# Attention probabilities in two parts: the second part written over its source, three heads in flight, sums two heads behind

## The chip, the cores and the metric

The kernel runs on one core of one Trainium2 chip. The metric is the device time of one execution in microseconds. The core has five engines with a queue each: TensorE (PE in the profile; its weight loads are listed as PEld), VectorE (DVE), ScalarE (ACT), GpSimd (POOL) and SyncE (SP), which issues nearly all DMAs. Each engine works through its own queue in order, and queues wait for one another through semaphores.

## The reference

One transformer block on x of 2048 tokens by 1024 channels, in fp32: a memory-augmented causal attention with 32 heads of 32 channels over four segments of 512 tokens, and then a token-mixing MLP. Both are modulated by a vector computed from c. Cut to the part that the change touches:

```python
for s in range(N):                      # N = 4 segments, L = 512
    logits = einsum("bhqd,bhkd->bhqk", qs, ks) * scale + mask
    p = softmax(logits, axis=-1)
    a_dot = einsum("bhqk,bhkd->bhqd", p, vs)
    num = einsum("bhld,bhde->bhle", phi(qs), M)
    den = einsum("bhld,bhd->bhl", phi(qs), z)[..., None] + 1e-6
    outs.append(g * num / den + (1.0 - g) * a_dot)
    M = M + einsum("bhld,bhle->bhde", phi(ks), vs)
    z = z + einsum("bhld->bhd", phi(ks))
o = stack(outs) @ wo                     # heads joined
x = x + ga * o                           # h = layernorm, modulated, before
x = x + gb * (W2 gelu(W1 layernorm(x)^T + b1) + b2)^T
```

## The kernel before

**Numbers in parts.** To keep fp32 accuracy at the rate of narrower matmuls, an operand is split into a rounded first part and the rest. A large product is then three matmuls: first by first, first by second, second by first (`kv_chunk`, L187; `q_chunk`, L198; L795; L925). `split` (L117) makes the two parts: a copy on ACT and a subtraction on DVE.

**Stages.** The start (to about 60 us) computes the modulation and the first normalized segment. The attention stage follows, then the output projection (`product`, L776) with the second normalization, and then the MLP (`mix`, L910) by a seven-product scheme, which fills the rest of the run from about 1160 us. The change lies in the attention stage alone.

**The attention stage.** The work is cut into 32 items `t`: two passes, in each the eight groups of four heads, in each two segments. Each item has four heads, so there are 128 heads `n = 4t + h`. The loop at L690 runs over `n`, and each iteration issues, in this order, `scores` of head n, `maxima` of head n + 3 (LEADS), `values` of head n - VL, and one of four pieces of `project` for the item eight heads ahead (LEADP). Side work that is planned for an iteration (weight splits, normalized token tiles, the modulation's other rows) follows, some of it held behind a marked instruction of head n on the same engine (`behind`, L504).

`project` (L380): pieces 0 and 1 each multiply half of the segment's tokens by the weights of k and v, 48 matmuls of 256 columns, into a bank of the tag pj (two banks), and copy k and v out (L400, L401, on ACT). A third copy from the same bank, L406, rounds v to bf16 into the tile `vp`; after piece 1 a DVE subtraction (L408) makes the rest, `r1`. Piece 2 transposes k, projects q, splits both into `sg` and, for the memory, computes phi of q and k. Its DMAs (`stack`, L370) put each head's parts of q and k beside each other in `sk`. Piece 3 stacks the fourth head, makes v's second part (L442, ACT) and third part (L443, DVE), and runs `memory` (L446), which reads and updates M and z.

`maxima` (L473): the masked scores of one head, three banks in turn of the tag s1 (two banks), each reduced by DVE to row maxima (L485); for each pair of heads the maxima are transposed, split and sent by DMA into two further rows of `sk` (L498).

`scores` (L512): the transposed scores with the maxima already subtracted by those rows, three banks of the tag s2 (two banks), and an exponential of each on ACT (L520, L523, L527) into `p32`, 1280 fp32 columns. POOL clears the upper triangles (L530). ACT rounds all of it to fp16, the first part (L532), and POOL subtracts that from p32, in two halves of 640 columns, into the second part (L534).

`values` (L536): ten blocks for the first part (97 columns: a column of ones for the row sums, and v's three parts) and ten for the second part (65 columns) are summed in one bank, the only one of the tag pv. DVE inverts the sums (L551), adds the parts (L553) and scales (L555), and POOL adds the memory's share (L558). After the fourth head the item is transposed, copied (L565) and stored (L566) in `oT`, from which L779 loads the operands of the output projection.

**Buffers.** Until now p32 has two buffers (5,120 bytes a partition each), and the two parts share the tile `ph` with two buffers (5,120 bytes each). A p32 buffer is free when POOL has subtracted, a ph buffer when TensorE has summed. `vp` has three buffers, `v32` one, `r1` one of its own.

**What sets the order.** The program gives each engine's instructions and their data; the framework's planner simulates the program with a cost model before the run and fixes the order on each queue: by the order of the program, with instructions further on drawn forward when those ahead are not ready in that simulation. On the chip each queue then runs in that order.

Of the kernel before, what the change touches and what calls it, by code (L numbers as in the profile page):

```python
# [7 lines left out]
F32 = mybir.dt.float32  # L8
F32R = mybir.dt.float32r
F16 = mybir.dt.float16  # L10
BF16 = mybir.dt.bfloat16
AF = mybir.ActivationFunctionType
ALU = mybir.AluOpType
# [5 lines left out]
P = 128  # L19
# [8 lines left out]
NV = 97  # L28
FT = F // P
LEADP, LEADS, NSK = 8, 3, 8  # L30
XB = 4
VL = 1
PHB = 2
P32B = 2
ML0 = 36
HB = 3
WO0 = 65
# [6 lines left out]
def attention_and_mlp(ctx, tc, x, wq, wkv, wo, beta, w1, b1, w2, b2, c, wm_a, wm_b, out):  # L44
    nc = tc.nc
    V, A, G, T, SY = nc.vector, nc.scalar, nc.gpsimd, nc.tensor, nc.sync
# [17 lines left out]
    a = par.__enter__()  # L64
# [257 lines left out]
    for i in range(2):  # L322
        ps = bank("s2", 2, f"scps{i}")
# [20 lines left out]
    pj = prj.__enter__()  # L344
    late = tc.tile_pool(name="late", bufs=1, reuse_waits="tile")
    b = late.__enter__()
# [33 lines left out]
    def project(t, piece):  # L380
        pr, g, seg = its[t]
        if piece == 0:
            st[t] = {}
        w = W[pr, g]
        hp = [hpages[seg, ct] for ct in range(NK)]
        d = st[t]
        if piece in (0, 1):
            if piece == 0:
                d["k32"] = pj.tile([P, 4, 128], F32, tag="k32", bufs=1, name=f"k32_{t}")
                d["v32"] = pj.tile([P, 4, 132], F32, tag="v32", bufs=1, name=f"v32_{t}")  # L390
                G.memset(d["v32"][:, :, 128:132], 1.0)
            half = piece
            k32, v32 = d["k32"], d["v32"]
            if t:
                ps = two_tiles(bank("pj", 2, f"nps{t}_{half}"))
                for k in range(NK):
                    kv_chunk(w, hp[k], half, k, ps)
            else:
                ps = two_tiles(first[half])
            A.copy(k32[:, 2 * half:2 * half + 2], ps[:, :, 0:128])  # L400
            A.copy(v32[:, 2 * half:2 * half + 2, 0:128], ps[:, :, 128:256])  # L401
            if half == 0:
                d["vp"] = b.tile([P, 4, 4, NV], BF16, tag="vp", bufs=3, name=f"vp{t}")
                G.memset(d["vp"][:, :, :, 0:1], 1.0)
                d["r1"] = pj.tile([P, 4, 4, 32], F32, tag="r1", bufs=1, name=f"r1_{t}")
            A.copy(d["vp"][:, 2 * half:2 * half + 2, :, 1:33], ps[:, :, 128:256].rearrange("p a (h e) -> p a h e", h=4))  # L406
            if half:
                V.tensor_tensor(d["r1"], v32[:, :, 0:128].rearrange("p a (h e) -> p a h e", h=4), d["vp"][:, :, :, 1:33],  # L408
                                op=ALU.subtract)
        elif piece == 2:  # L410
            k32 = d["k32"]
            d["sg"] = sg = pj.tile([P, 4, L], F32R, tag="sg", bufs=1, name=f"sg{t}")
            ps = bank("pj", 2, f"kps{t}")
            for i in range(4):
                T.transpose(ps[:, 128 * i:128 * i + 128], k32[:, i], ident)
            split(sg[:, 2:4], ps, A, V)
            if t:
                ps = bank("pj", 2, f"qps{t}")
                for k in range(NK):
                    q_chunk(w, hp[k], k, ps)  # L420
            else:
                ps = first[2]
            split(sg[:, 0:2], ps, A, V)
            if seg:
                r = pj.tile([P, L], F32, tag="tmp", bufs=2, name=f"rq{t}")
                A.activation(r, ps, AF.Relu, scale=-1.0)
                A.activation(r, r, AF.Exp, scale=-1.0)
                d["pq"] = pj.tile([P, L], F32, tag="pq", bufs=1, name=f"pq{t}")
                V.scalar_tensor_tensor(d["pq"], ps, 0.0, r, op0=ALU.max, op1=ALU.add)
            if seg < 3:  # L430
                r = pj.tile([P, L], F32, tag="tmp", bufs=2, name=f"rk{t}")
                kf = k32.rearrange("p a n -> p (a n)")
                A.activation(r, kf, AF.Relu, scale=-1.0)
                A.activation(r, r, AF.Exp, scale=-1.0)
                d["pk"] = pj.tile([P, 4, 128], F32, tag="pk", bufs=1, name=f"pk{t}")
                V.scalar_tensor_tensor(d["pk"].rearrange("p a n -> p (a n)"), kf, 0.0, r, op0=ALU.max, op1=ALU.add)
            for h in range(3):
                stack(t, h)
        else:
            stack(t, 3)  # L440
            vp, r1 = d["vp"], d["r1"]
            A.copy(vp[:, :, :, 33:65], r1)  # L442
            V.tensor_tensor(vp[:, :, :, 65:97], r1, vp[:, :, :, 33:65], op=ALU.subtract)  # L443
            memory(t)
# [56 lines left out]
    marks = {}  # L501
# [10 lines left out]
    def scores(t, h):  # L512
        d = st[t]
        n = 4 * t + h
        q, k = d["sk", h][:, 0], d["sk", h][:, 1]
        p32 = r_.tile([P, 1280], F32, tag="p32", bufs=P32B, name=f"p32_{t}_{h}")
        d["ph", h] = ph = r_.tile([P, 2, 1280], F16, tag="ph", bufs=PHB, name=f"ph{t}_{h}")
        b0 = bank("s2", 2, f"a0_{t}_{h}")
        T.matmul(b0, k[:, 0:128], q, start=True, stop=True)  # L519
        A.activation(p32[:, 0:512], b0, AF.Exp, scale=SCALE, bias=shift)  # L520
        b1_ = bank("s2", 2, f"a1_{t}_{h}")
        T.matmul(b1_[:, 0:384], k[:, 128:256], q[:, 128:512], start=True, stop=True)  # L522
        A.activation(p32[:, 512:896], b1_[:, 0:384], AF.Exp, scale=SCALE, bias=shift)  # L523
        b2_ = bank("s2", 2, f"a2_{t}_{h}")
        T.matmul(b2_[:, 0:128], k[:, 384:512], q[:, 384:512], start=True, stop=True)
        T.matmul(b2_[:, 128:384], k[:, 256:384], q[:, 256:512], start=True, stop=True)  # L526
        A.activation(p32[:, 896:1280], b2_[:, 0:384], AF.Exp, scale=SCALE, bias=shift)  # L527
        for base, step in ((0, 512), (896, 128)):
            w = bass.AP(tensor=p32.tensor, offset=p32.offset + base, ap=[p32.ap[0], [step, 2], [1, 128]])
            G.affine_select(w, w, pattern=[[0, 2], [1, 128]], compare_op=ALU.is_ge, fill=0.0, base=0,  # L530
                            channel_multiplier=-1)
        marks[n, "A"] = A.copy(ph[:, 0], p32)  # L532
        for c in (slice(0, 640), slice(640, 1280)):
            marks[n, "G"] = G.tensor_tensor(ph[:, 1, c], p32[:, c], ph[:, 0, c], op=ALU.subtract)  # L534

    def values(t, h):  # L536
        pr, g, seg = its[t]
        d = st[t]
        am, ph = d["am"], d["ph", h]
        pv = bank("pv", 1, f"pv{t}_{h}").rearrange("p (a n) -> p a n", a=4)  # L540
        col = {0: lambda i: 128 * i, 1: lambda i: 512 + 128 * (i - 1), 2: lambda i: 1024 + 128 * (i - 2),
               3: lambda i: 896}
        n = 0
        for part, w in ((0, NV), (1, 65)):
            for i in range(4):
                for j in range(i + 1):
                    o = col[j](i)
                    T.matmul(pv[:, i, 0:w], ph[:, part, o:o + 128], d["vp"][:, j, h, 0:w], start=(n == 0),  # L548
                             stop=(n == 19), skip_group_check=True)
                    n += 1  # L550
        V.reciprocal(pv[:, :, 0], pv[:, :, 0])  # L551
        red = r_.tile([P, 4, 32], F32, tag="red", bufs=2, name=f"red{t}_{h}")
        V.tensor_reduce(red, pv[:, :, 1:97].rearrange("p a (c e) -> p a e c", c=3), axis=AX.X, op=ALU.add)  # L553
        ah = am[:, :, 32 * h:32 * h + 32]
        V.scalar_tensor_tensor(red if seg else ah, red, gate[:, 1, 4 * g + h:4 * g + h + 1],  # L555
                               pv[:, :, 0:1].to_broadcast([P, 4, 32]), op0=ALU.mult, op1=ALU.mult)
        if seg:
            G.tensor_tensor(ah, ah, red, op=ALU.add)  # L558
        if h < 3:
            return  # L560
        ps = bank("ms", 1, f"ops{t}")
        for i in range(4):
            T.transpose(ps[:, 128 * i:128 * i + 128], am[:, i], ident)
        ot = r_.tile([P, L], F32, tag="ot", bufs=1, name=f"ot{t}")
        A.copy(ot, ps)  # L565
        SY.dma_start(oT[g, :, L * seg:L * seg + L], ot)  # L566
        del st[t]
# [47 lines left out]
    with tc.issue_after(last_wm.ins):  # L615
        _, exp, _, normed_v = seg_load(1)
# [25 lines left out]
    r_ = right.__enter__()  # L642
# [32 lines left out]
    for g in range(2, NG):  # L675
        n = 8 * g - 13
# [5 lines left out]
    for j in range(32):  # L682
        n = ML0 + 2 * j + (8 if j >= 8 else 0)
        later(n, lambda j=j: mod_fetch(j), n + (2 if j < 8 else 1), lambda r, j=j: mod_late(j, r), "V")
    plan(WO0 - 3, lambda: spread(gaw, 0))
    for i in range(8):
        n = WO0 + WOS * i
        later(n, lambda i=i: wo_fetch(i), n + 1, lambda r, i=i: wo_split(i, r), "G")

    for n in range(-LEADS, 4 * NI + VL):  # L690
        at(scores, n)
        at(maxima, n + LEADS)
        at(values, n - VL)
        m = n + LEADP
        if 0 <= m + 4 < 4 * NI:
            t = (m + 4) // 4
# [12 lines left out]
        if 4 * NI - 5 <= m < 4 * NI + 3:  # L709
            i = m - 4 * NI + 5  # L710
# [21 lines left out]
    w = cw_pool.__enter__()  # L732
# [120 lines left out]
    for products, tt in (((0, 1), 0), ((2,), 1), ((3, 4, 8), 8), ((9,), 9), ((10,), 2), ((11,), 10), ((12,), 3),  # L853
# [5 lines left out]
        for i in products:  # L859
            if i > 1:  # L860
                f = product(i)
# [283 lines left out]
```

## Time and profile before

| what | us |
| --- | --- |
| median of three runs | 2234.29 |
| fastest of them | 2233.22 |
| the profiled execution, its own time | 2231.97 |
| its span, first to last instruction | 2230.3 |
| TensorE busy in the span | 2194.8 (98%) |
| DVE, ACT, POOL busy | 1675.3, 1136.8, 721.0 |

One of the three runs took 4396.86 us, which the median leaves aside. All times that are read from the trace belong to the one profiled execution; its own time lies 1.7 us above its span. The busy time of TensorE is partly modelled, since matmuls are pipelined, so that its idle time in a stage tells more than its busy share. A row of a view by groups names line, engine, operation, tiles and shapes, then the count, the busy us, the mean ns of one, and the engine's idle time just before with what ended it.

### The profile page before, as it was taken

How to read it: one execution, taken by the hardware profiler on the slowest of the kernel's cores; microseconds unless marked ns; L12 is line 12 of the kernel's file. 1: busy time of each engine (PE TensorE's matmuls, PEld its weight loads, DVE VectorE, ACT ScalarE, POOL GpSimd, SP SyncE). 2: the span in 40 equal slices, each digit the busy share in tenths (PEclk: the TensorE clock that was granted, in tenths of full speed). 3: DMA queues.
4: the chain of work that ended last, by engine and by line, in shares of the span. 5: the costliest groups of instructions: out<-in, count | busy, mean ns of one | idle time of the engine just before them, and what ended most of it. 6: DMA issues, size and time to landing. Idle time of an engine off the chain costs nothing.

```text
span 2230.3 us, 38268 instructions
## 1 busy us (share of the span) xinstructions
PE 2194.8 (98%) x13786; PEld 1885.9 (85%) x13786; DVE 1675.3 (75%) x3762; ACT 1136.8 (51%) x2082; POOL 721.0 (32%) x831
## 2 busy tenths in 40 slices
PE   8999999999999999999999999999999999999999
PEld 5889898889989989888888888888888888888887
DVE  7677677766767777655858766888888886969687
ACT  5477777756666656645636533533334242424232
POOL 2176666656766767654001200033330000000000
PEclk9999999999999999999999999999999999999999
DMA  7657565697656566765654586655556541414134
GB/s 285 191 170 212 161 191 155 202 293 220 187 165 199 178 199 181 214 189 180 218 198 178 223 322 258 245 221 221 206 204 224 204 146 62 151 57 146 57 123 151
DMA packets 175185, 423.05 MB, mean 190 GB/s; under 512 B 17524, under 2 KB 71828, under 8 KB 166036
## 3 DMA queue, kind: packets, MB, share of 16 engines
q1 hardware_dynamic: 174996, 420.61, 57.4%
q8 instruction: 109, 1.79, 0.3%
q14 instruction: 80, 0.66, 0.1%
HBM read 244.62 MB, written 125.06 MB: 166 GB/s over the span
## 4 chain that ended last, share of the span: by engine, by line
PE 87%; DVE 5%; DMA 3%; ACT 2%; POOL 2%; issue 1%; SPq 0%; ACTq 0%; DVEq 0%; POOLq 0%
PE mx L925 47%; PE nps L194 12%; PE po L795 7%; PE qps L202 7%; PE pv L548 3%; PE a L519 1%; POOL ph L534 1%; PE sz L483 1%; PE sx L483 1%; PE rd L455 1%; PE a L522 1%; PE sy L483 1%; PE up L465 1%; PE a L526 1%; ACT ph L532 1%
## 5 line engine op out<-in xcount | busy, mean ns | idle before, releaser
L925 PE MATMUL mx<-bU,sp 128*128 128x512 f32 x2352 | 534.2, 389 | 0.9 <-DVE ac L932 0.9
L925 PEld LDWEIGHTS mx<-bU,sp 128*128 128x128 f32 x2352 | 441.4, 188 | 93.2 <-issue 1.3
L194 PE MATMUL nps<-wv,h 128*128 128x256 f32 x3072 | 437.2, 282 | 1.3 <-DVE h L124 0.7
L121 ACT CAST sp<-wr 128x384 fp32r<-128x384 f32 (+2 forms) x408 | 217.3, 545 | 432.7 <-PE mx L925 355.4
L534 POOL TENSOR_TENSOR ph<-p,ph 128x640 f16<-128x640 f32 x256 | 381.2, 1510 | 155.1 <-ACT ph L532 150.8
L925 PE MATMUL mx<-bA,sp 128*128 128x512 f32 x1764 | 430.5, 389 | 0.0
L194 PEld LDWEIGHTS nps<-wv,h 128*128 128x128 f32 x3072 | 404.6, 189 | 8.7 <-DVE h L124 2.0
L925 PEld LDWEIGHTS mx<-bA,sp 128*128 128x128 f32 x1764 | 331.2, 188 | 68.6
L124 DVE TENSOR_TENSOR sp<-wr,sp 128x384 fp32r<-128x384 f32 (+2 forms) x408 | 259.7, 647 | 29.1 <-ACT sp L121 28.8
L932 DVE TENSOR_TENSOR ac<-mx,ac 128x512 f32<-128x512 f32 x280 | 189.7, 686 | 83.9 <-PE mx L925 83.5
L202 PE MATMUL qps<-h,wq 128*128 128x512 f32 x768 | 200.5, 403 | 0.4
L532 ACT CAST ph<-p 128x1280 f16<-128x1280 f32 x128 | 160.9, 1259 | 41.7 <-POOL p L530 41.3
L795 PE MATMUL po<-wo,ots 128*128 128x512 f32 x768 | 179.8, 390 | 0.6 <-DVE x L798 0.6
L795 PEld LDWEIGHTS po<-wo,ots 128*128 128x128 f32 x768 | 143.6, 188 | 30.1 <-DVE x L798 0.9
L202 PEld LDWEIGHTS qps<-h,wq 128*128 128x128 f32 x768 | 143.9, 193 | 29.0 <-ACT vp L406 1.4
L925 PE MATMUL mx<-bB,sp 128*128 128x512 f32 x588 | 164.0, 389 | 0.0
L530 POOL TENSOR_SCALAR_AFFINE_SELECT p<-p 128x256 f32<-128x256 f32 x256 | 121.3, 484 | 103.1 <-ACT p L527 51.8
L548 PE MATMUL pv<-vp,ph 128*128 128x97 bf16 (+1 forms) x2560 | 142.0, 201 | 6.5 <-DVE red L555 3.1
L548 PEld LDWEIGHTS <-ph 128*128 128x128 f16 x2560 | 113.9, 98 | 28.1 <-issue 13.3
L925 PEld LDWEIGHTS mx<-bB,sp 128*128 128x128 f32 x588 | 110.4, 188 | 22.9
L485 DVE CUSTOM_DVE_ANT_0 sx<-sx,mask 128x128 f32<-128x128 f32 (+1 forms) x256 | 93.7, 366 | 41.8 <-PE sx L483 39.5
L932 DVE TENSOR_TENSOR cc<-mx,cc 128x512 f32<-128x512 f32 x140 | 94.9, 684 | 39.6 <-PE mx L925 39.3
(207 smaller groups left out, 3149.7 us busy)
## 6 DMA issues: line engine op xcount, KB each, us to landing
sk<-sg SPq DMA_DIRECT2D x384, 128.0 KB
wr<-in_w_dram SPq DMA_DIRECT2D x28, 1024.0 KB
wr<-in_w_dram SPq DMA_DIRECT2D x32, 768.0 KB
bstu<-ucd SPq DMA_DIRECT2D x28, 768.0 KB
wsp<-wv SPq DMA_DIRECT2D x32, 512.0 KB
rawm<-in_wm_b_dram SPq DMA_DIRECT2D x32, 512.0 KB
wv<-wsp SPq DMA_DIRECT2D x32, 512.0 KB
pcd<-cc SPq DMA_DIRECT2D x14, 1024.0 KB
```

What stands on the lines that cost most here:

```text
L121: last_hi[0] = A.copy(hi, src)
L124: return lo_eng.tensor_tensor(lo, src, hi.bitcast(F32), op=ALU.subtract)
L194: T.matmul(ps[:, aa], h[:, j, 128 * tt:128 * tt + 128], wt[:, i, o:o + 256], start=(n == 0), stop=(n >= 6 * NK - 2), skip_group_check=True)
L202: T.matmul(ps, wt[:, i, o:o + 128], h[:, j], start=(k + n == 0), stop=(3 * k + n == 3 * NK - 1))
L485: marks[4 * t + h - LEADS, "V"] = V.tensor_tensor_reduce(o, o, mask[:, 384 - 128 * i:], 1.0, -3.0e38, op0=ALU.add, op1=ALU.max, accum_out= ...
L530: G.affine_select(w, w, pattern=[[0, 2], [1, 128]], compare_op=ALU.is_ge, fill=0.0, base=0, channel_multiplier=-1)
L532: marks[n, "A"] = A.copy(ph[:, 0], p32)
L534: marks[n, "G"] = G.tensor_tensor(ph[:, 1, c], p32[:, c], ph[:, 0, c], op=ALU.subtract)
L548: T.matmul(pv[:, i, 0:w], ph[:, part, o:o + 128], d["vp"][:, j, h, 0:w], start=(n == 0), stop=(n == 19), skip_group_check=True)
L795: T.matmul(ps, os_[:, i, P * ct:P * ct + P], wop[ct, nh][:, j], start=(n == 0), stop=(n == 3 * NK - 1))
L925: T.matmul(ps, ops[q][:, i, P * k:P * k + P], b[:, j], start=(m == 0 and first), stop=(m == 3 * nk - 1), skip_group_check=True)
L932: V.tensor_tensor(d, ps, d, op=ALU.add)
```

## The change

VL goes from 1 to 2: `values` of a head is issued two iterations after its `scores`. The second part of the probabilities is no longer a tile half of its own: POOL writes it, as fp16, over the first half of the bytes of the p32 buffer that it is reading. p32 and the first part have three buffers each (5,120 and 2,560 bytes a partition). A p32 buffer is therefore free when TensorE has summed the head.

v's three bf16 parts are all made in piece 3 of `project`, from the fp32 copy `v32` in SBUF: the memset of the ones, one ACT copy of all four token tiles instead of two from the PSUM bank, and the subtraction. `r1` takes a buffer of the tag tmp, which has two and is shared with the scratch of phi.

```diff
-VL = 1
-PHB = 2
-P32B = 2
+VL = 2
...
-            if half == 0:
-                d["vp"] = b.tile([P, 4, 4, NV], BF16, tag="vp", bufs=3, name=f"vp{t}")
-                G.memset(d["vp"][:, :, :, 0:1], 1.0)
-                d["r1"] = pj.tile([P, 4, 4, 32], F32, tag="r1", bufs=1, name=f"r1_{t}")
-            A.copy(d["vp"][:, 2 * half:2 * half + 2, :, 1:33], ps[:, :, 128:256].rearrange("p a (h e) -> p a h e", h=4))
-            if half:
-                V.tensor_tensor(d["r1"], v32[:, :, 0:128].rearrange("p a (h e) -> p a h e", h=4), d["vp"][:, :, :, 1:33],
-                                op=ALU.subtract)
...
             stack(t, 3)
-            vp, r1 = d["vp"], d["r1"]
+            v = d["v32"][:, :, 0:128].rearrange("p a (h e) -> p a h e", h=4)
+            vp = d["vp"] = b.tile([P, 4, 4, NV], BF16, tag="vp", bufs=3, name=f"vp{t}")
+            r1 = pj.tile([P, 4, 4, 32], F32, tag="tmp", bufs=2, name=f"r1_{t}")
+            G.memset(vp[:, :, :, 0:1], 1.0)
+            A.copy(vp[:, :, :, 1:33], v)
+            V.tensor_tensor(r1, v, vp[:, :, :, 1:33], op=ALU.subtract)
             A.copy(vp[:, :, :, 33:65], r1)
...
-        p32 = r_.tile([P, 1280], F32, tag="p32", bufs=P32B, name=f"p32_{t}_{h}")
-        d["ph", h] = ph = r_.tile([P, 2, 1280], F16, tag="ph", bufs=PHB, name=f"ph{t}_{h}")
+        p32 = r_.tile([P, 1280], F32, tag="p32", bufs=3, name=f"p32_{t}_{h}")
+        hi, lo = r_.tile([P, 1280], F16, tag="ph", bufs=3, name=f"ph{t}_{h}"), p32.bitcast(F16)[:, 0:1280]
+        d["ph", h] = hi, lo
...
-        marks[n, "A"] = A.copy(ph[:, 0], p32)
+        marks[n, "A"] = A.copy(hi, p32)
         for c in (slice(0, 640), slice(640, 1280)):
-            marks[n, "G"] = G.tensor_tensor(ph[:, 1, c], p32[:, c], ph[:, 0, c], op=ALU.subtract)
+            marks[n, "G"] = G.tensor_tensor(lo[:, c], p32[:, c], hi[:, c], op=ALU.subtract)
...
-                    T.matmul(pv[:, i, 0:w], ph[:, part, o:o + 128], d["vp"][:, j, h, 0:w], start=(n == 0),
+                    T.matmul(pv[:, i, 0:w], ph[part][:, o:o + 128], d["vp"][:, j, h, 0:w], start=(n == 0),
```

## The prediction

> **What bounds the kernel now.** I read the page first, for the whole span, and then the view of busy time by stretch, cut at the places where the stages change: the start, the attention stage in which the change lies (100 to 956 us), its tail under the first output products, and the rest.
>
> ```profile
> span 2230.3 us, 38268 instructions
> ...
> PE 2194.8 (98%) x13786; PEld 1885.9 (85%) x13786; DVE 1675.3 (75%) x3762; ACT 1136.8 (51%) x2082; POOL 721.0 (32%) x831
> ```
>
> ```profile
> 0.00:60.00 60.00, 48.94 (x272) 31.59 (x272) 43.85 (x89) 31.45 (x53) 13.56 (x49) 1.00 0.74 278
> 60.00:100.00 40.00, 39.14 (x276) 35.84 (x277) 27.43 (x76) 15.30 (x33) 3.35 (x6) 1.00 0.71 229
> 100.00:956.00 856.00, 837.53 (x7442) 767.93 (x7441) 618.05 (x1827) 579.07 (x1059) 556.71 (x660) 0.99 0.65 192
> 956.00:1050.00 94.00, 93.45 (x617) 77.62 (x616) 53.62 (x156) 47.61 (x80) 48.13 (x54) 1.00 0.58 191
> 1050.00:2230.00 1180.00, 1175.72 (x5185) 972.93 (x5183) 932.31 (x1617) 463.40 (x859) 99.26 (x64) 1.00 0.52 182
> ```
>
> The columns are length, busy us of PE, weight loads, DVE, ACT and POOL, then the granted clock. The reader is to see that TensorE bounds even the attention stage: it is idle for 856.00 - 837.53 = 18.5 us of it, while POOL is busy for 557 and ACT for 579. The change removes no matmul. So whatever it does to POOL or ACT, it can win only these 18.5 us, and what the clock loses there. The clock is lost in five stretches, which I asked for by themselves:
>
> ```profile
> 124.90:131.70 6.80, 6.56 (x28) 5.24 (x29) 4.32 (x11) 5.12 (x11) 5.62 (x8) 0.50 0.94 289
> 247.70:251.10 3.40, 3.40 (x13) 2.92 (x14) 2.88 (x11) 2.68 (x6) 0.00 (x0) 0.50 0.38 151
> 367.20:370.60 3.40, 3.40 (x11) 2.81 (x12) 3.40 (x9) 2.07 (x6) 3.26 (x3) 0.50 0.46 114
> 428.60:432.00 3.40, 3.40 (x14) 2.92 (x12) 3.40 (x12) 3.25 (x7) 1.68 (x2) 0.51 0.46 186
> 807.50:810.90 3.40, 3.40 (x13) 2.98 (x12) 3.40 (x8) 1.61 (x4) 3.32 (x3) 0.50 0.59 160
> ```
>
> They sum to 6.8 + 4 x 3.4 = 20.4 us at half clock, or 10.2 us lost. The ceiling of any gain is 18.5 + 10.2 = 28.7 us, 1.3% of the run. Next, who made TensorE wait in that stage (the view of waits, TensorE alone, 100 to 956 us; total us, times, longest):
>
> ```profile
> PE pv L548 <- DVE red L555: 3.1, 2, 1.9
> PE sy L483 <- DVE mx L485: 3.0, 4, 1.5
> PE a L519 <- DMA sk<-nt: 2.3, 3, 1.6
> PE pv L548 <- POOL ph L534: 2.0, 4, 0.7
> PE sz L483 <- DVE mx L485: 1.7, 3, 1.3
> PE pv L548 <- ACT p L523: 1.3, 1, 1.3
> PE hpl L262 <- ACT gaw L241: 1.2, 1, 1.2
> PE rd L455 <- DVE pq L429: 0.7, 1, 0.7
> PE a L519 <- ACT p L523: 0.5, 1, 0.5
> PE nmps L491 <- DVE tm L470: 0.3, 1, 0.3
> PE a L519 <- ACT vp L406: 0.3, 1, 0.3
> PE kps L415 <- ACT vp L406: 0.2, 1, 0.2
> PE a L525 <- ACT p L520: 0.2, 1, 0.2
> ```
>
> The waits that the change aims at, sums waiting for POOL's second parts, are 2.0 us in all. The large waits are those of the other engines, and they cost time only where they reach TensorE:
>
> ```profile
> ACT p L520 <- POOL ph L534: 18.7, 16, 2.5
> ```
>
> ```profile
> POOL vp L404 <- PE pv L548: 13.2, 13, 3.2
> ```
>
> ```profile
> DVE pv L551 <- PE pv L548: 60.6, 59, 4.3
> ```
>
> **The change part by part.** The costs of its operations are in the view of groups (line, engine, operation, count | busy us, mean ns | idle before):
>
> ```profile
> L534 POOL TENSOR_TENSOR ph<-p,ph 128x640 f16<-128x640 f32 x256 | 381.2, 1510 | 155.1 <-ACT ph L532 150.8 <-DVE mx L485 2.6 <-DVE am L555 1.4
> ...
> L406 ACT CAST vp<-nps 128x256 bf16<-128x256 f32 x64 | 23.6, 390 | 0.4 <-PE pv L548 0.4
> ...
> L656 POOL TENSOR_TENSOR wor<-wor,gaw 128x512 f32<-128x512 f32 x16 | 22.6, 1432 | 0.0
> ...
> L442 ACT CAST vp<-r 128x512 bf16<-128x512 f32 x32 | 20.4, 637 | 10.6 <-DVE r L408 10.3
> L270 POOL TENSOR_TENSOR gaw<-gaw,hix 128x512 fp32r<-128x512 f32 x16 | 20.2, 1284 | 20.5 <-ACT hix L268 20.5
> ```
>
> *Second parts over the fp32 numbers.* The same 256 subtractions of 640 columns; only the place of the result differs. A 16-bit result over its own fp32 source doesn't occur in the trace. The nearest rows are POOL's subtraction and product that write over a source: 1284/512 = 2.51 and 1432/512 = 2.80 ns an element, against 1510/640 = 2.36. If writing in place is what makes them slower, a head pays 1280 x 0.15 to 0.44 ns = 0.2 to 0.56 us of POOL; the other end is nothing. I take nothing, since those two rows also write 32-bit results. Even 0.56 us x 128 = 72 us fits into POOL's idle 856 - 557 = 299 us, and the sums now come a head later; without that cover it would be late in each head.
>
> *Sums two heads behind, three heads in flight.* The order on each queue is fixed before the run by a planner, and the sums move by one iteration, about (1050 - 100)/128 = 7.4 us. Their second parts are then ready, so the waits of pv for POOL (2.0) and ACT (1.3) go: **-3.3**. The 3.1 us behind DVE's last reading of the pv bank stay, since that bank stays single. The 4.7 us of the score maxima (3.0 + 1.7) wait for a bank that DVE frees, and DVE stands at L551 for the sums in 59 heads, 60.6 us in all; with value matmuls that no longer stop half way, these shorten. Bounds: all 4.7, or none, if DVE's queue is held by its other work; I take half, **-2.3**. The added wait: a p32 buffer is now freed by TensorE's last value matmul of its head, not by POOL. Behind L520 in ACT's queue stand the other exponentials, the first-part copy and the copies that free the projection banks, for which TensorE waits. Today that place waits 18.7 us for POOL with two buffers. I cost the wait with three at nothing: its cover is the third head of 7.4 us. What it costs without that is the third rival.
>
> *v's parts in the last piece.* Two ACT copies out of PSUM become one out of SBUF: 32 x (2 x 390 - 637 ns) = 4.6 us of ACT, off the path. The projection bank is free one reader (0.39 us) sooner, so the 0.3 + 0.2 us behind L406 go: **-0.5**. POOL's memset no longer waits 13.2 us for the sums. Moved into piece 3 with the copy are one DVE subtraction and the memset, no DMA; the stack's three DMAs of the fourth head are issued ahead of them as before, and the memory products' queue positions follow them. v32 is now read until piece 3, so the next v copy (ACT) and POOL's memset of its ones wait for that subtraction; that is bounded by nothing and, should ACT stand for a whole L442 copy each time, 32 x 0.64 = 20 us of ACT, which has 856 - 579 = 277 us idle. I take nothing.
>
> *The tail.* The last sums come one head later. The tail's order of time, to see what needs them:
>
> ```profile
> 1018.74 0.32 SPq L566 DMA_DIRECT2D oT<-ot  x1
> ...
> 1021.14 0.37 SPq L779 DMA_DIRECT2D otr<-oT  x1
> ...
> 1026.46 0.68 DVE L124 TENSOR_TENSOR ots<-otr,ots 128x512 fp32r<-128x512 f32 x1
> ...
> 1027.06 0.18 DVE L551 RECIPROCAL pv<-pv 128x4 f32<-128x4 f32 x1
> ...
> 1033.96 0.19 DVE L551 RECIPROCAL pv<-pv 128x4 f32<-128x4 f32 x1 [1.95 <-PE pv L548]
> ...
> 1037.92 1.14 ACT L121 CAST ots<-otr 128x512 fp32r<-128x512 f32 x2 [2.24 <-PE po L795]
> ```
>
> The store at 1018.74 releases the load for the first product that needs the third segment; its operand is complete at 1027.1, and its matmuls begin when the product before frees its buffer, at 1037.9. That is 10.8 us of slack against one head of 1033.96 - 1027.06 = 6.9 us: nothing, with 3.9 us to spare. SP's queue holds these loads in order; the later ones start from freed buffers and not from sums.
>
> *The clock.* The stage with the waits is the one with the drops: 0.99 there, 1.00 in the row after 1050 us, where TensorE waits hardly at all. Of the 16.8 us that the thirteen rows of waits name, the terms above take 3.3 + 2.3 + 0.5 = 6.1, a third of the 18.5 us idle. I let a third of the four stretches after the start's go with them: 4 x 3.4 / 2 / 3 = **-2.3** (bounds: nothing, and all 10.2).
>
> The sum is -6.1 - 2.3 = -8.4 us. Against the profiled execution's 2231.97 us it gives 2223.6; the median shown is 2234.29, 2.3 us above that execution, so the time to expect is 2225.9, say 2226 us. My own bounds for it: with no help from the maxima and the clock -3.8, with 4.7 of the one and half of the other -13.6, so 2221 to 2231.
>
> **The rivals.** *The clock doesn't answer.* If the clock falls by its own schedule, or only after longer idleness than these waits, term four is nothing: 2234.3 - 6.1 = 2228. For it: the first 60 us, in which TensorE is idle for 60.00 - 48.94 = 11.1 us, show a clock of 1.00. Against it: the even 1.00 after 1050 us. The Trainium skill ("TensorE: Matmul & The Clock Gate", sections "HAM oscillation" and "Why this matters for your kernels") names idle gaps above about 3 us as what halves the clock. By that rule no wait of this stage, the longest 1.9 us, could cause a drop, and the sum would be this rival's; the trace has five drops without such a gap and so speaks against it, and the same page also tells of drops from many short idles.
>
> *Nothing changes.* TensorE stays full, the planner's new order trades 6 us of waits for others of the same size, or the pace is set elsewhere so that no third head is ever in flight: 2234, within 3 us. For it: of the 16.8 us of waits only 2.0 + 1.3 + 0.3 + 0.2 = 3.8 us are named by this change's own operations.
>
> *ACT stands behind TensorE* (slower). A p32 buffer lives from its first exponential to its last value matmul, and if the planner places the sums so late that they end after the exponential three heads on would begin, ACT stops, and with it the copies that free banks. Price: if each head waits as the 16 do today, 18.7/16 = 1.17 us x 128 = 150 us of ACT. TensorE's waits for p are 1.3 + 0.5 + 0.2 = 2.0 us where ACT's wait is 18.7, so a ninth comes through: +16 us, 2250; if a quarter came through, +37, 2271. It decides from the point where the sums stand over 7.4 us behind their place. Against it: TensorE takes the sums as soon as their iteration comes.
>
> *All idleness goes*: -28.7, 2206. For it: DVE, ACT and POOL all loosen at once. Against: the waits for L555 (3.1) and for the DMA of the maxima (2.3) are not touched.
>
> **How the numbers follow.** Forecast 0.37, the clock rival 0.13, nothing 0.20, slower 0.21, all idleness 0.09. The range reaches from the last rival's inner half, 2208, to just above the slow one's first price, 2254, and leaves out about half of the one and a third to a half of the other, under 2 in 10. Over 2% is 45 us (about what a measurement of this kernel can tell from no change): a gain of that size is above the ceiling of 28.7, so 0.02 for what the views don't show; a loss needs almost a third of ACT's 150 us on TensorE, 0.04.
>
> **What would show it.** In the changed profile the attention stage's TensorE idle should be near 12 us, the waits of pv for POOL and of L519 and L415 for v's copy gone, L551's wait under 60 us, one copy of 0.64 us in place of two of 0.39, POOL's subtraction still near 1510 ns, and L520 waiting for pv under 10 us. A row of ACT waiting for pv for tens of us, a product waiting for its operand near 1037 us, or more half-clock stretches than five would make me wrong.

## The result, and the profile after

The changed kernel is faster by a fifth of a percent: the ratio of its times to those of the kernel before is 0.9979, with a 95% interval of 0.9971 to 0.9987. That is 4.7 us of 2232.4 us, between 2.9 and 6.5 us (medians of fourteen runs each: 2227.44 and 2232.4 us; the fourteen of before include the three that the prediction saw). The forecast was 8.4 us, with a range of 2208 to 2254 us. The two profiled executions have spans of 2230.3 and 2224.9 us, 5.4 us apart. A few executions ran far longer (4396.86 us for one of before, 3252.9 us for the profiled one of the kernel with in-place second parts and two buffers, 2407.76 us for one with two buffers of the first parts), and the ratios leave them out.

All of it is won before the MLP starts. The view of one tile gives the first and last start of its matmuls (median ns between the slashes); these are the MLP's first operands, in the kernel before and then in the changed one:

```profile
L925 PE MATMUL mx<-bA,sp x1764: 389/389/389, 1158.8 to 1698.9; 128*128 128x512 f32 x196
```

```profile
L921 PE MATMUL mx<-bA,sp x1764: 389/389/389, 1153.3 to 1693.5; 128*128 128x512 f32 x196
```

The first starts 5.5 us earlier, the last 5.4. Next, the changed kernel's busy time in the stretches that the prediction used, and its half-clock stretches (line numbers are now a few lower than before):

```profile
0.00:60.00 60.00, 49.66 (x273) 31.97 (x273) 43.92 (x89) 31.98 (x53) 13.57 (x49) 1.00 0.75 280
60.00:100.00 40.00, 39.61 (x285) 36.92 (x286) 26.73 (x77) 15.81 (x33) 3.88 (x5) 1.00 0.69 226
100.00:956.00 856.00, 836.61 (x7459) 767.17 (x7458) 613.70 (x1829) 577.30 (x1031) 565.34 (x663) 0.99 0.65 194
956.00:1050.00 94.00, 93.98 (x617) 76.67 (x616) 55.56 (x160) 48.24 (x82) 43.87 (x50) 1.00 0.56 182
```

```profile
133.00:136.40 3.40, 3.40 (x23) 3.19 (x23) 2.76 (x3) 3.40 (x8) 3.13 (x3) 0.50 1.00 260
453.90:464.10 10.20, 8.81 (x46) 7.90 (x47) 7.73 (x26) 4.41 (x9) 4.43 (x9) 0.50 0.99 371
```

TensorE's idle time up to 1050 us was 11.06 + 0.86 + 18.47 + 0.55 = 30.9 us and is now 10.34 + 0.39 + 19.39 + 0.02 = 30.1. In the stage itself it did not fall but rose by 0.9 us. The clock gives more: two half-clock stretches of 3.4 + 10.2 = 13.6 us in place of five of 20.4, so 3.4 us less lost, or 4.0 if half of TensorE's busy time in them is counted (half of 20.2 against half of 12.2). Together that is 4.2 to 4.8 of the 5.5 us; the rest lies in what the profile calls busy. This is one execution of each. The mean granted clock is on record for every other run too: 0.9957 over 67 runs of the kernel before, taken beside the experiments, and 0.9967 over the fourteen of the changed kernel. A difference of 0.001 of 2230 us is some 2 us, so that nearly half of the 4.7 us goes with the clock.

Why the idle time stayed is seen in the waits of TensorE in the stage:

```profile
PE a L515 <- DMA sk<-nt: 4.1, 5, 1.4
PE up L460 <- DVE am L454: 3.8, 3, 3.5
PE a L521 <- ACT p L516: 2.4, 3, 1.0
PE sy L478 <- DVE mx L480: 1.9, 2, 1.2
PE sy L478 <- DVE rdd L453: 1.1, 1, 1.1
PE pv L544 <- DVE red L551: 0.9, 2, 0.8
...
PE kps L405 <- ACT k L398: 0.7, 1, 0.7
...
PE kps L405 <- ACT v L399: 0.6, 1, 0.6
...
PE sx L478 <- DVE mx L480: 0.4, 1, 0.4
PE pv L544 <- POOL p L530: 0.3, 1, 0.3
```

The waits that the change aims at did go: sums for POOL from 2.0 to 0.3 us, sums for ACT from 1.3 to nothing, maxima for DVE's reductions from 4.7 to 2.3 (and one waits 1.1 us until DVE ends L453, 3.4 in all). The sums' wait for DVE's last reading, which was to stay at 3.1 us, is 0.9. Others stand in their place: memory products for DVE (3.8), score matmuls for ACT's exponential (2.4, was 0.2), and for the maxima's DMA (4.1, was 2.3). All rows of the view together come to 19.3 us, where they were 16.8.

The groups of operations that the change touched:

```profile
L530 POOL TENSOR_TENSOR p<-p,ph 128x640 f16<-128x640 f32 x256 | 380.2, 1485 | 138.5 <-ACT ph L528 134.5
...
L547 DVE RECIPROCAL pv<-pv 128x4 f32<-128x4 f32 x128 | 24.1, 188 | 54.2 <-PE pv L544 53.5
...
L435 ACT CAST vp<-v 128x512 bf16<-128x512 f32 x32 | 20.3, 634 | 1.3 <-PE pv L544 0.8
```

POOL's subtraction over its own source takes 1485 ns, where it took 1510. DVE's wait at the first reading of the sums fell from 69.2 to 53.5 us over the whole run, and v's copy is one of 634 ns. ACT's first exponential, which waited 18.7 us for POOL in the stage, now waits for it once, and nowhere in the stage for the sums:

```profile
ACT p L516 <- POOL p L526: 0.4, 1, 0.4
```

### The profile page after: what moved, and what is told of

It reads as the page before. It is cut to its first block, busy times and chain, and to the rows that moved or that the text cites. A ratio compares the mean times of both kernels' runs of the same rounds, so it can differ in the third digit from the quotient of the medians.

```text
span 2224.9 us, 38052 instructions
## 1 busy us (share of the span) xinstructions
PE 2190.3 (98%) x13786; PEld 1881.0 (85%) x13786; DVE 1666.7 (75%) x3762; ACT 1135.7 (51%) x2050; POOL 725.8 (33%) x831
## 4 chain that ended last, share of the span: by engine, by line
PE 87%; DVE 5%; DMA 3%; ACT 2%; POOL 1%; issue 1%; SPq 0%; DVEq 0%; ACTq 0%
PE mx L921 48%; PE nps L192 11%; PE po L791 8%; PE qps L200 7%; PE pv L544 3%; PE a L515 1%; PE sz L478 1%; PE sx L478 1%; DMA sk<-nt 1%; PE up L460 1%; PE a L518 1%; POOL p L530 1%; PE a L522 1%; PE sy L478 1%; PE rd L450 1%
## 5 line engine op out<-in xcount | busy, mean ns | idle before, releaser
L192 PE MATMUL nps<-wv,h 128*128 128x256 f32 x3072 | 431.2, 283 | 1.6 <-DVE h L122 0.7
L530 POOL TENSOR_TENSOR p<-p,ph 128x640 f16<-128x640 f32 x256 | 380.2, 1485 | 138.5 <-ACT ph L528 134.5
L122 DVE TENSOR_TENSOR sp<-wr,sp 128x384 fp32r<-128x384 f32 (+2 forms) x408 | 259.8, 648 | 24.7 <-ACT sp L119 24.4
L791 PEld LDWEIGHTS po<-wo,ots 128*128 128x128 f32 x768 | 142.7, 188 | 28.7
L526 POOL TENSOR_SCALAR_AFFINE_SELECT p<-p 128x256 f32<-128x256 f32 x256 | 134.1, 529 | 81.8 <-ACT p L523 53.9
L480 DVE CUSTOM_DVE_ANT_0 sz<-sz,mask 128x512 f32<-128x512 f32 x128 | 89.1, 696 | 52.0 <-PE sz L478 49.5
L516 ACT ACTIVATE p<-a,shift 128x512 f32<-128x512 f32 x128 | 88.4, 691 | 41.2 <-PE a L515 40.4
```

The lines of the kernel that those rows point to most:

```text
L122: return lo_eng.tensor_tensor(lo, src, hi.bitcast(F32), op=ALU.subtract)
L192: T.matmul(ps[:, aa], h[:, j, 128 * tt:128 * tt + 128], wt[:, i, o:o + 256], start=(n == 0), stop=(n >= 6 * NK - 2), skip_group_check=True)
L480: marks[4 * t + h - LEADS, "V"] = V.tensor_tensor_reduce(o, o, mask[:, 384 - 128 * i:], 1.0, -3.0e38, op0=ALU.add, op1=ALU.max, accum_out= ...
L530: marks[n, "G"] = G.tensor_tensor(lo[:, c], p32[:, c], hi[:, c], op=ALU.subtract)
L791: T.matmul(ps, os_[:, i, P * ct:P * ct + P], wop[ct, nh][:, j], start=(n == 0), stop=(n == 3 * NK - 1))
```

## The experiments

My theory was that the gain comes from the later place of the sums, with the third head as its cover. The rivals were that one of the other parts, the third buffer by itself, or a new order of the planner's makes it. The first four kernels take the change apart. All ratios are to the kernel before, run beside each.

**v's parts alone.** The kernel before with

```diff
-            if half == 0:
-                d["vp"] = b.tile([P, 4, 4, NV], BF16, tag="vp", bufs=3, name=f"vp{t}")
...
+            A.copy(vp[:, :, :, 1:33], v)
+            V.tensor_tensor(r1, v, vp[:, :, :, 1:33], op=ALU.subtract)
```

> The kernel before, with only v's parts moved into the last piece (sums one head behind, two buffers, second parts in their own place). If the gain comes from the sums' later place (the prediction), this is worth the 0.5 us of its own term: 2232 us, ratio 0.999 to 1.001. If the gain comes from the earlier release of the projection bank, it shows most of the 5 us here: ratio 0.998. If the sums one head behind now collide with the later buffers of vp, it is slower, up to the 13.2 us that POOL waited for that tile.

Measured: 2235.13 us, ratio 1.0005 (0.9994 to 1.0016). The part by itself wins nothing that can be seen; it is not the source. The planner made a new order for it: in the traces, by the names of their tiles, 4879 of TensorE's 13,786 weight loads stand in another place than in the kernel before.

**Second parts in place, two buffers.** The kernel before with only

```diff
-        d["ph", h] = ph = r_.tile([P, 2, 1280], F16, tag="ph", bufs=PHB, name=f"ph{t}_{h}")
+        hi, lo = r_.tile([P, 1280], F16, tag="ph", bufs=PHB, name=f"ph{t}_{h}"), p32.bitcast(F16)[:, 0:1280]
+        d["ph", h] = hi, lo
```

> The kernel before, with only the second parts written over their source; still two buffers, sums one head behind, v's parts as before. POOL's subtraction should stay near 1510 ns if writing in place is free, and go up by 100 to 280 ns each if it is not. A buffer is now freed by TensorE's sums and not by POOL, with no third head: ACT's first exponential (L520 of before) should wait for the sums for more than the 18.7 us it waited for POOL; if a ninth of it reaches TensorE, as in the prediction's slow rival, the time rises by 2 to 16 us (ratio 1.001 to 1.007). If TensorE is covered, 1.000.

Measured: 2252.59 us, ratio 1.0089 (1.0073 to 1.0105): 20 us slower, more than the 16 us that I expected at most. Writing in place is free for POOL, as the row of the changed kernel shows, but it isn't free for the kernel. The likely cause is that the buffer is held until the sums are done; the trace that shows such waits is that of the next kernel.

**Two buffers, sums two heads behind.** The changed kernel with

```diff
-        p32 = r_.tile([P, 1280], F32, tag="p32", bufs=3, name=f"p32_{t}_{h}")
-        hi, lo = r_.tile([P, 1280], F16, tag="ph", bufs=3, name=f"ph{t}_{h}"), p32.bitcast(F16)[:, 0:1280]
+        p32 = r_.tile([P, 1280], F32, tag="p32", bufs=2, name=f"p32_{t}_{h}")
+        hi, lo = r_.tile([P, 1280], F16, tag="ph", bufs=2, name=f"ph{t}_{h}"), p32.bitcast(F16)[:, 0:1280]
```

> The changed kernel with two buffers each in place of three: sums two heads behind, but only two heads can be in flight. This is the condition of the prediction's slow rival: the exponentials two heads on wait for sums. By that rival's price (a ninth of ACT's waits) it is 16 us slower than before or more: ratio 1.007 to 1.02. If the planner places the sums by their readiness and not by the loop's order, the two heads cost little: 0.998 to 1.002.

Measured: 2256.18 us, ratio 1.0100 (1.0084 to 1.0116), 22 us slower. Its waits of ACT in the stage, and its busy time there:

```profile
ACT p L516 <- PE pv L544: 26.6, 24, 3.6
```

```profile
100.00:956.00 856.00, 829.70 (x7262) 753.31 (x7261) 606.63 (x1789) 563.60 (x1006) 543.52 (x639) 0.98 0.64 190
```

ACT's first exponential waits for the sums, as the slow rival says, where it waited 18.7 us for POOL in the kernel before. TensorE is idle for 26.3 us in place of 19.4, at a lower clock, and gets 197 fewer matmuls done in the same stretch than in the changed kernel.

**Three buffers, sums one head behind.** The changed kernel with

```diff
-VL = 2
+VL = 1
```

> The changed kernel, but sums one head behind (VL = 1), with three buffers and v's parts in the last piece. If the later sums are what helps, this loses most of the 4.7 us: ratio to the kernel before 0.999 to 1.001, and TensorE again waits some us for POOL's second parts and ACT's first parts. If the third buffer alone helps, it stays at 0.998.

Measured: 2229.68 us, ratio 0.9987 (0.9978 to 0.9996). Without the later place of the sums the change gives 2.9 of the 4.7 us. What that place adds is 0.0008, and the two intervals overlap: it is not settled that it adds anything. How the 2.9 us come about stays open: TensorE's idle time in the stage is 856.00 - 834.66 = 21.3 us in this kernel, more than the 18.5 of before, and the mean clock of its twelve runs is 0.9957, against 0.9954 for the kernel before beside it. Its waits of the sums show how little there is to win by it:

```profile
PE pv L544 <- DVE red L551: 1.3, 3, 0.8
PE pv L544 <- ACT ph L528: 0.5, 1, 0.5
PE pv L544 <- POOL p L530: 0.3, 1, 0.3
```

With a third buffer the sums hardly wait for POOL or ACT even one head behind.

**Which third buffer.** The changed kernel with two buffers for the first parts:

```diff
-        hi, lo = r_.tile([P, 1280], F16, tag="ph", bufs=3, name=f"ph{t}_{h}"), p32.bitcast(F16)[:, 0:1280]
+        hi, lo = r_.tile([P, 1280], F16, tag="ph", bufs=2, name=f"ph{t}_{h}"), p32.bitcast(F16)[:, 0:1280]
```

> The changed kernel with two buffers in place of three for the first parts alone; the fp32 numbers keep three, sums two heads behind. A first part then waits for the sums two heads back, where in the order of the loop those sums come after it. If the buffer that matters is the one of the fp32 numbers, where the exponentials begin, this stays at 0.998 to 1.000. If both are needed, it falls back towards the kernel with two of each: 1.005 to 1.01.

Measured: 2232.59 us, ratio 0.9995 (0.9986 to 1.0004). The fp32 numbers' third buffer brings back nearly all of the 22 us, from 1.0100 to 0.9995; the first parts' third buffer is worth the last 0.0016, which carries the kernel below the one before (the intervals, from 0.9986 and to 0.9987, just touch).

**A new order by itself.** The kernel before with POOL's small memset moved to the last piece:

```diff
-                G.memset(d["vp"][:, :, :, 0:1], 1.0)
...
             vp, r1 = d["vp"], d["r1"]
+            G.memset(vp[:, :, :, 0:1], 1.0)
```

> The kernel before with one small thing moved: POOL's memset of the ones of vp (0.18 us, 32 times) is issued in the last piece and not in the first, so that POOL no longer waits for that tile, 13.2 us in all; the planner makes a new order for all of the stage. If a new order alone moves the time by as much as the change did, this differs from before by 3 us or more, either way. If orders of the same program are worth about the same, 0.999 to 1.001.

Measured: 2234.62 us, ratio 1.0003 (0.9993 to 1.0013). POOL's wait for that tile did not go away, which I had thought it would (13.4 us for the sums, against 13.2). The traces show why: the order on TensorE, DVE, ACT and SP is that of the kernel before, and on POOL one memset at the start has moved. So this run doesn't test new orders; it shows how well two nearly equal programs agree. The kernel with v's parts alone, whose order differs widely, is the one such trial, and its time doesn't move. One trial is no proof, but it gives no support to the view that new orders by themselves move this kernel by 5 us.

**What POOL's subtraction is worth.** In both kernels the subtraction is left out, and the second ten blocks of a sum read the first part again. In the changed kernel:

```diff
-        for c in (slice(0, 640), slice(640, 1280)):
-            marks[n, "G"] = G.tensor_tensor(lo[:, c], p32[:, c], hi[:, c], op=ALU.subtract)
...
-                    T.matmul(pv[:, i, 0:w], ph[part][:, o:o + 128], d["vp"][:, j, h, 0:w], start=(n == 0),
+                    T.matmul(pv[:, i, 0:w], ph[0][:, o:o + 128], d["vp"][:, j, h, 0:w], start=(n == 0),
```

> The kernel before without POOL's second parts: the subtraction is left out and both halves of the sums read the first part, so the matmuls are as many as before and 381 us of POOL's work are gone. This is the most that any cure of the sums' wait for POOL could give with two heads in flight. By the view of waits of before, TensorE waits 2.0 us for POOL, and the ceiling of the stage is 28.7 us: 2225 to 2231 us, ratio 0.996 to 0.999. If POOL's chain held the stage by more than the waits show, 0.99.

> The changed kernel without POOL's second parts (both halves of the sums read the first part). If the change has taken POOL's chain off the path, as the prediction has it, nothing is left to win from POOL here: within 3 us of the changed kernel, ratio to before 0.997 to 0.999. If the chain still counts, it gains as much again as the other kernel without them does.

Measured: the kernel before falls to 2219.41 us, ratio 0.9938 (0.9925 to 0.9951), and the changed one to 2207.47 us, ratio 0.9886 (0.9872 to 0.9900). The main branch of both expectations was wrong, and the alternative that each names came nearer. Two microseconds of waits stood for 14 us, and the changed kernel, in which TensorE waits 0.3 us for POOL, gains 20 us. Nor is the gain seen in idle time: in the kernel before without the subtraction, TensorE is idle for 19.6 us of the stage, more than the 18.5 of before; its busy time in the whole run falls from 2194.8 to 2183.0 us for the same 13,786 matmuls. Its half-clock stretches sum to 17.0 us in place of 20.4, which accounts for less than 2 us of that.

```profile
PE 2183.0 (98%) x13786; PEld 1881.5 (85%) x13786; DVE 1621.9 (73%) x3762; ACT 1136.8 (51%) x2082; POOL 336.9 (15%) x575
```

The busy time of DVE shows one way by which POOL reaches TensorE without a wait that names it. These are the weight splits on DVE in the stage (mean ns after the comma), in the kernel before and in the changed kernel without the subtraction:

```profile
L124 DVE TENSOR_TENSOR wv<-rawv,wv 128x512 fp32r<-128x512 f32 x24 | 33.6, 1419 | 4.8 <-ACT wv L121 4.8
```

```profile
L122 DVE TENSOR_TENSOR wv<-rawv,wv 128x512 fp32r<-128x512 f32 x24 | 16.6, 717 | 2.5 <-ACT wv L119 2.3
```

```profile
100.00:956.00 856.00, 847.39 (x7604) 775.94 (x7603) 583.92 (x1873) 587.00 (x1048) 218.32 (x434) 1.00 0.67 199
```

The same operation takes twice as long on the average in the kernel with POOL's subtraction, and the changed kernel's idle time of TensorE in the stage is 8.6 us without it (DVE's busy time in the whole run: 1666.7 us in the changed kernel, 1625.0 without the subtraction). Of the weight splits of v and q in the last trace, the 22 beside which POOL does nothing take 671 to 697 ns; the rest stand beside its triangles and other work. The splits of q, which have the same shape but read one source from a PSUM bank, take the same time with the subtraction (first row, kernel before) and without it (second, changed kernel):

```profile
L124 DVE TENSOR_TENSOR sg<-qps,sg 128x512 fp32r<-128x512 f32 x29 | 19.9, 686 | 3.2 <-ACT sg L121 3.2
```

```profile
L122 DVE TENSOR_TENSOR sg<-qps,sg 128x512 fp32r<-128x512 f32 x29 | 19.9, 687 | 10.7 <-ACT sg L119 10.7
```

In the kernel before, 17 of the splits of q and k lie beside POOL's subtraction for nine tenths of their time or more, and take 669 to 692 ns. So it is the operation with two sources in SBUF that POOL lengthens. The Trainium skill ("SBUF — State Buffer", section "Who interferes with whom") says that a DVE instruction with two SBUF inputs contends with a GpSimd instruction that reads SBUF, and not with one that only writes it. That gives a test.

**POOL writes only.** The changed kernel, each subtraction replaced by a memset of the whole fp32 buffer (the second parts are then zero):

```diff
-            marks[n, "G"] = G.tensor_tensor(lo[:, c], p32[:, c], hi[:, c], op=ALU.subtract)
+            marks[n, "G"] = G.memset(p32, 0.0)
```

> The changed kernel with each of POOL's two subtractions of a head replaced by a memset of the whole fp32 buffer, which reads nothing from SBUF and should take about 1.3 us in place of 1.4 (an estimate from the memset of the mask, 512 columns in 0.53 us): the second parts are zero, and POOL's place in the chain and in its queue stays. Leaving the subtraction out gave the changed kernel 20 us. If those come from POOL's time in the chain, this stays near the changed kernel: 2225 to 2229 us, ratio 0.997 to 0.999. If they come from DVE's operations with two SBUF sources, which stand longer beside POOL's subtraction (the weight split 1419 ns beside it, 708 ns without), it goes most of the way to the kernel without subtraction: 2208 to 2215 us, ratio 0.988 to 0.992, with DVE's busy time in the stage near 580 us in place of 614.

Measured: 2216.57 us, ratio 0.9933 (0.9918 to 0.9947). The groups of POOL and of the weight split on DVE in the stage:

```profile
L530 POOL MEMSET p<- 128x1280 f32 x240 | 280.2, 1168 | 139.7 <-ACT ph L528 134.6 <-DVE rawm L573 1.4
```

```profile
L122 DVE TENSOR_TENSOR wv<-rawv,wv 128x512 fp32r<-128x512 f32 x24 | 16.6, 716 | 2.6 <-ACT wv L119 2.6
```

The split is back at 716 ns though POOL's memsets are busy for 280 us there. Of the weight splits of v and q in this trace, the 23 that stand beside a memset alone take 673 to 693 ns, and four beside POOL's triangles alone, which read SBUF, 793 to 917. What lengthens them is POOL's reading, as that section of the Trainium skill has it. The time goes about half of the way, 10 of 20 us, between my two expectations. The memset is also shorter than the subtraction (1168 ns against 1492 in the stage), so part of the 10 us may be POOL's shorter chain; the two were not separated further. The other 10 us are not explained: besides POOL's work, the kernel without the subtraction also lacks the sums' reading of the fp32 buffer, which is then free sooner.

**The subtraction moved to DVE**, half of it and all of it (each half over its own source):

```diff
-        for c in (slice(0, 640), slice(640, 1280)):
-            marks[n, "G"] = G.tensor_tensor(lo[:, c], p32[:, c], hi[:, c], op=ALU.subtract)
+        marks[n, "G"] = G.tensor_tensor(lo[:, 0:640], p32[:, 0:640], hi[:, 0:640], op=ALU.subtract)
+        V.tensor_tensor(lo[:, 1280:1920], p32[:, 640:1280], hi[:, 640:1280], op=ALU.subtract)
```

> The changed kernel with the second 640 columns of the second part subtracted by DVE, each half in place over its own source. POOL is left with half its subtractions, 190 us less, the chain of a head is shorter by some 0.7 us, and DVE gets 128 x 0.7 to 1.4 us = 90 to 180 us more, on some 614 of 856 us. If POOL's chain and its reads beside DVE are what is left to win, this beats both kernels: 2215 to 2224 us, ratio 0.992 to 0.996. If DVE's queue is the closer limit (its maxima are what TensorE waits for), it is slower than the changed kernel: 2235 to 2260 us, 1.001 to 1.012.

> The changed kernel with the whole second part subtracted by DVE in one instruction of 1280 columns, and POOL left with the triangles. DVE gets 128 x 1.4 us = 180 us more and loses up to 40 us of standing beside POOL: some 750 of 856 us. If POOL's reads are the whole of what is left, 2215 us, ratio 0.992. If DVE's queue becomes the bound of the stage, slower: 2240 to 2280 us, 1.004 to 1.02.

Measured: 2239.39 us, ratio 1.0031 (1.0020 to 1.0042), and 2258.76 us, ratio 1.0109 (1.0093 to 1.0126). DVE's part in the one and the other, in the stage:

```profile
L530 DVE TENSOR_TENSOR p<-p,ph 128x640 f16<-128x640 f32 x116 | 138.6, 1194 | 32.9 <-ACT ph L528 32.6
```

```profile
L529 DVE TENSOR_TENSOR p<-p,ph 128x1280 f16<-128x1280 f32 x114 | 176.4, 1547 | 24.8 <-ACT ph L528 24.2
```

```profile
PE sz L478 <- DVE mx L480: 4.7, 6, 1.7
PE pv L543 <- DVE red L550: 3.6, 5, 1.4
```

Half the columns cost DVE 1194 ns beside POOL, where all of them without POOL's half cost 1547. The last fence is TensorE's waits with all of it on DVE: they are for the maxima and for the reading of the sums. Without POOL's part the second parts are ready in less of an engine's time (1547 ns against twice 1492) and the kernel is still slower, which speaks for DVE's queue as the closer limit.

**Weight splits moved to POOL**, the other direction:

```diff
-            split(w, r[:, 512 * i:512 * i + 512], A, V)
+            split(w, r[:, 512 * i:512 * i + 512], A, G if g > 1 else V)
```

> The changed kernel with the second parts of the weights of k, v and q (36 subtractions of two SBUF sources in the stage, 51 us of DVE's 614) made by POOL in place of DVE, for the head groups from the third on. Moving 82 us more onto DVE made the kernel 12 us slower; if DVE's queue is the limit behind TensorE, 51 us less should make it some 7 us faster, less what 36 x 1.4 = 50 us more cost POOL: 2219 to 2224 us, ratio 0.994 to 0.997, better than both kernels. If POOL's chain is as close a limit as DVE's queue, it stays at 0.998, or is slower: up to 2235 us, 1.001.

Measured: 2225.26 us, ratio 0.9958 (0.9944 to 0.9971).

```profile
100.00:956.00 856.00, 838.63 (x7462) 768.46 (x7461) 578.50 (x1799) 576.93 (x1030) 598.64 (x699) 0.99 0.66 194
```

DVE has 35 us less in the stage and POOL 33 us more. It is faster than the kernel before; against the changed kernel's 0.9979 (0.9971 to 0.9987) the intervals just touch, so that it is better by 0.2% if at all.

**The clock over all of these.** The mean granted clock of the profiled execution of the changed kernel without the subtraction, the one with POOL's memset, the one with two buffers, and the one with all of it on DVE:

```profile
core 0: 2204.8 us, clock 1.000
```

```profile
core 0: 2210.1 us, clock 1.000
```

```profile
core 0: 2250.7 us, clock 0.994
```

```profile
core 0: 2251.6 us, clock 0.993
```

The two kernels with the least idle time in the stage (8.6 and 12.4 us) run at full clock in these executions, and the two slow ones (26.3 and 31.7 us) have the lower clock. Over all their runs the mean clocks are 1.000, 0.998, 0.994 and 0.992. The other profiles fit less well: the kernel before has 18.5 us of idle time and 20.4 of half clock in the stage, the one with half of the subtraction on DVE 25.9 and 13.6.

## Why the prediction was right or wrong

The direction and the range held, and the gain is a little over half of the forecast; the range also holds no change at all. The account of where it comes from held in part, and that the time came out as near as this owes something to luck: of the 6.1 us that were to leave TensorE's idle time, 0.8 did up to the MLP and none in the stage, and the clock gave its 2.3 us, more or less, without them.

*The ceiling: 28.7.* The prediction took idle time and lost clock for all that the change could win. The kernel before without the subtraction shows that this isn't so: it is 14 us faster with no less idle time in the stage, and TensorE's busy time falls by 11.8 us. What in the busy time shrinks is not shown; the ends of matmuls are modelled there.

*Second parts over the fp32 numbers: nothing.* Right for POOL, 1485 ns against 1510. But as a step of the change it costs 0.9%, shown by the kernel with that step alone; I had put this under the added wait.

*The added wait, covered by the third head: nothing.* Right, and the most important line of the sum: ACT's first exponential waits nowhere in the stage for the sums. The cover was named, and its loss measured: 20 and 22 us with two buffers, where the slow rival's price was 16. The price was near by two errors that cancel: ACT's exponential waits for the sums 26.6 us in the stage and not 150, and nearly as much as it waits is lost, not a ninth. How it comes through is not in TensorE's waits alone: against the changed kernel, 7 us of idle time are seen and 27.2 us at half clock in place of 13.6, which is some 7 us more; the MLP begins 24.4 us later, and the rest lies in the busy time.

*Sums two heads behind: -3.3, and -2.3 for the maxima.* The named waits went nearly as worked out: 3.3 to 0.3 us, and 4.7 to 2.3 us, or to 3.4 with the wait that ends at L453. The step that failed is that these microseconds leave TensorE's idle time. New waits of 3.8 us for the memory products and 2.4 us for exponentials came, and the stage's idle time is 19.4 us, not near 12. Nor is the place of the sums what brings it: with VL = 1 and three buffers 2.9 us are there already, at an idle time of 21.3 us.

*v's parts: -0.5.* The 0.5 us behind v's third reader became 0.7 + 0.6 us behind k's and v's copies, and the part alone measures as nothing.

*The tail: nothing.* Right, by where the whole gain lies: the MLP begins 5.5 us earlier, with 0.02 us of idle time from 956 to 1050 us.

*The clock: -2.3.* It is -3.4 in the profiled executions, the largest term that is seen there, and some -2 by the mean clocks of all runs. That this is near the forecast is in part luck, since its reason was a third of the idle time, which did not go. The rival in which the clock doesn't answer lost ground: the profiles above with the least idle time have the full clock and those with the most the lowest. That is a correlation, and a loose one in between. The order of time of the changed kernel shows the end of that stage's longest wait:

```profile
455.29 1.00 PE L460 MATMUL up<-v,pk 128*128 128x132 f32 x3 [3.48 <-DVE am L454]
```

The 10.2 us stretch begins at 453.9, in this wait of 3.48 us for DVE, when it had lasted 2.1 us. The changed kernel's other drop, at 133.0, has no wait above 0.65 us in the 5 us before it, and the longest wait in the stage of before, with its five drops, is 1.94 us. The rule that the prediction cited from "TensorE: Matmul & The Clock Gate" in the Trainium skill, a gap above about 3 us, fits one drop of the seven by the length of the gap, and not by the moment at which the clock falls.

*All idleness goes: 2206.* Only a kernel with POOL's subtraction left out came there (2207), and not by this way: it keeps 8.6 us of idle time in the stage. I had excluded it for the changed kernel with the right reason, the waits for DVE and for the DMA, but not seen that POOL's reads stand behind DVE's.

*What a measurement can tell.* The prediction put this at about 45 us. The interval measured here is less than 2 us to either side.

## What to carry to other kernels

A result written over its source makes the source's buffer live as long as the result: count the longer life as a wait and look for the buffer that covers it before counting the memory saved; here the saved bytes (twice 2,560 a partition) pay for just that buffer of 5,120, and the first parts' third buffer costs 2,560 more. Where one engine is full, the waits that name an engine don't tell what that engine is worth: leave its work out once and measure, and note what else that frees. One engine's reads of SBUF can lengthen another engine's operations on two SBUF sources without any wait in the list; compare the same operation's mean duration beside the other engine and alone.

## What was not expected of the hardware

POOL's subtraction, waited for by TensorE for 2.0 us, is worth 14 us to the kernel before and 20 us to the changed one. DVE's subtraction of 512 columns with two SBUF sources takes 1419 ns on the average in the kernel before, 671 to 697 ns with POOL idle, and 673 to 693 ns beside a POOL that only writes; with one source in PSUM it takes 680 to 687 ns on the average, with or without POOL's subtraction. A DVE subtraction of 640 columns beside POOL's of the same buffer takes 1194 ns, while 1280 columns with POOL on its triangles take 1547.
